# Two weight pieces joined in turn, convolution taps in token halves, and a new step list for the first phase

## The chip, the cores and the metric

The program runs on one core of a Trainium2 chip. Its time is the device time of one execution in microseconds (us). A core has five engines that run side by side, each through its own queue in order: PE (matmul), DVE (vector), ACT (scalar), POOL (GpSimd) and SP (which issues the DMAs here). They wait for one another through semaphores.

## The reference

Attention without a causal mask in two forms (on tokens averaged by 4, and in a local band), their sum as the input of a gated layer, and a mixer over tokens and channels:

```
out_up    = repeat(softmax(q_d k_d^T / 8) v_d, 4)        # q_d, k_d, v_d: means of 4 tokens
out_local = softmax(where(|i-j| < 4, q k^T / 8, -1e9)) v
x   = out_up + out_local                                 # B 4, S 576, 8 heads x 64 = 512 channels
gate = sigmoid(sum_k conv_w[k] * x shifted by 4-k tokens)  # 5 taps per channel
y   = (gate * (x @ w_val)) @ w_out                       # 512 x 512 each
u   = y + (relu(y^T @ w_tok1) @ w_tok2)^T                # tokens 576 -> 256 -> 576
out = u + relu(u @ w_ch1) @ w_ch2                        # channels 512 -> 1536 -> 512
```

The seven weight arrays (`w_val`, `conv_w`, `w_out`, `w_tok1`, `w_tok2`, `w_ch1`, `w_ch2`) arrive as the bits of 64-bit floats.

## The kernel before, in words

Channels lie on the partitions, tokens along the free dimension. A product is made of three fp32r matmuls (L278 to L280, `mm3`): each operand is split into a high and a low part, the high part by a copy on ACT, the low part by a subtraction on DVE (or POOL).

**Weights.** A weight comes in pieces of 128 x 256. `fetch_bits` loads the 64-bit words of a piece into one of three raw buffers (tag `w64`, `NWD` = 3). `join_bits` makes fp32 bits of it with three DVE instructions, each of which reads what the one ahead wrote: a shift and mask (L152), the sign (L153), the low word (L155). Then ACT writes the high part and DVE the low part.

**First phase** (`start`, batch 0). The attention of batch 0, its convolution and the 16 pieces of `w_val` (0 to 7) and `w_out` (8 to 15; an even piece holds columns 0 to 255 of a row block, an odd one the others) run by the string `ORDER`. Each word of it is a step with a number: `qk`, `va`, `vw`, `wf`, `cwf` are loads on SP; `wj` joins a piece, `wl` makes its low part, `S` sums tokens by 4, `md`/`ml` take maxima, `rd`/`rl` normalise, `xf` adds the two attention outputs into x, `ca`/`cb`/`cc` are convolution taps, `xl` the low part of x (all on DVE); `wh`, `ed`, `ela`, `elb`, `cd`, `cl`, `up`, `g`, `xh`, `sg` are on ACT; `D`, `L`, `T`, `O` are on PE, and `z` puts in dummy matmuls that keep PE going. PE, ACT, DVE and SP follow this list word for word. A matmul `p_val` (x times `w_val`) of batch 0 follows the list, and DVE multiplies its result with the gate (`y`, L749); the `p_x` matmuls (y times `w_out`) come next, and need the 16th piece's low part in the end.

**Later phases.** Only PE's order is written out there (`mix` places side work such as attention of batches 1 to 3 and weight steps between the products, by nominal times on PE); the other engines follow a scheduler's priorities. `ch1_new` prepares `w_ch1` (24 pieces, 12 columns blocks `f`), `load_w` the token weights, `ch2_new` prepares `w_ch2` (24 pieces). The convolution of batches 1 to 3 is `conv`: one multiplication (L457) and four taps (L462), each over all 576 tokens and each reading the sum that the tap ahead wrote.

Of the kernel before, what the change touches and what calls it, by code (L numbers as in the profile page):

```python
# [21 lines left out]
NHP = H // 2  # L22
# [15 lines left out]
LAG = 2  # L38
# [15 lines left out]
NW0, NW1 = 8, 3  # L54
# [5 lines left out]
TAG0 = {"sc_d": "as", "sc_l": "m", "o_d": "n", "o_l": "n"}  # L60
# [25 lines left out]
def kernel(ctx, tc, qk, vw, v4, w_val, conv_w, w_out, w_tok1, w_tok2, w_ch1, w_ch2, out):  # L86
# [32 lines left out]
    def busy(n):  # L119
        for _ in range(n):  # L120
            p = T(ps, [128, 512], F32, "ao", BANKS["ao"], name="idle_ps")
            nc.tensor.matmul(p, lhsT=idle, rhs=idle.unsqueeze(1).to_broadcast([128, 4, 128]), start=True, stop=True)

# [25 lines left out]
    def join_bits(x, n, rows, full=None):  # L149
        a = T(sb, [128, n], I32, "wa", NWD, name="wa")[0:rows]  # L150
        low, high = x[:, :, 0], x[:, :, 1]
        nc.vector.tensor_scalar(a, high, 3, 0x3FFFFFF8, ALU.logical_shift_left, ALU.bitwise_and)  # L152
        nc.vector.scalar_tensor_tensor(out=a, in0=high, scalar=-0x40000000, in1=a,  # L153
                                       op0=ALU.bitwise_and, op1=ALU.bitwise_or)
        nc.vector.scalar_tensor_tensor(out=a if full is None else full.bitcast(I32), in0=low, scalar=29, in1=a,  # L155
                                       op0=ALU.logical_shift_right, op1=ALU.bitwise_or)
        return a

    def decode(src, n, rows, hi, lo, shape=None, keep=0, lo_eng=nc.vector):
        a = join_bits(fetch_bits(src, n, rows, shape), n, rows)  # L160

        def split():
            nc.scalar.activation(out=hi, in_=a.bitcast(F32), func=AF.Copy)
            lo_eng.tensor_tensor(out=lo, in0=a.bitcast(F32), in1=hi.bitcast(F32), op=ALU.subtract)  # L164

        if not keep:
            flush()
        pending.append(split)

    def load_w(key, pieces, tag, bufs, parts=None):  # L170

        for j, group in enumerate(pieces):
            n = group[0][1].shape[1]
            hi, lo = parts or [T(sb, [128, len(group), n], F32R, tag, bufs, name=f"{key}{j}_{p}") for p in ("hi", "lo")]
            for i, (rows, src) in enumerate(group):
                for c in range(0, n, WB):
                    e = min(n, c + WB)
                    decode(src[:, c:e], e - c, rows, hi[0:rows, i, c:e], lo[0:rows, i, c:e])
                wt[key].append((hi[:, i, :], lo[:, i, :]))
                yield  # L180
# [21 lines left out]
    def ch1_new(f):  # L202
# [41 lines left out]
    def ch2_new():  # L244
# [10 lines left out]
        for k in range(NP):  # L255
            w = wt["ch2", k] = [next(slots) for _ in range(7)]
            x = []
            for f, c in ((k, WB), (k + NP, WB), (k, 0), (k + NP, 0)):
                x.append(whole("pt", NPT))
                join_bits(fetch_bits(w_ch2[f * 128:f * 128 + 128, c:c + WB], WB, 128), WB, 128, full=x[-1])  # L260
                with behind_pace():
                    for _ in range(2):
                        if splits:
                            part(*splits.pop(0))
                yield
# [46 lines left out]
    def softmax(parts, e, scale, mult):  # L312
# [17 lines left out]
        mult.tensor_tensor(out=e, in0=e, in1=bc(sm, w), op=ALU.mult)  # L330

    def attention(b):
# [3 lines left out]
        early = lambda: tc.high_priority(offset=PRI) if b else nullcontext()  # L336
        mult = nc.gpsimd if b else nc.vector

        def bank(shape, name, tag=None):
            if b:  # L340
                tag = "as" if name[:2] == "sc" else "ao"
            else:
                tag = tag or TAG0.get(name, "ao")
            return T(ps, shape, F32, tag, BANKS[tag], name=name)

        def sums(hp):
# [7 lines left out]
            if b == 0:  # L354
                d["vd"] = [w[:, r] for r in range(4)]
                return
# [5 lines left out]
        def low_scores(hp):  # L362
# [9 lines left out]
            softmax(parts, e, 0.125 / 16.0, mult)  # L372
# [31 lines left out]
        def loc_scores(hp):  # L404
# [16 lines left out]
            softmax(parts, e, 0.125, mult)  # L421
# [50 lines left out]
        if b:

            hpd[0] = load(b, 0)
            hpd[0]["v"] = load_v(b, 0)
            yield
            sums(0)
            for i in range(NHP + 1):
                if i < NHP:
                    low_scores(i)  # L480
                    yield
                if i:
                    low_turn(i - 1)
                    yield
                if i < NHP:
                    loc_scores(i)
                    yield
                if i + 1 < NHP:
                    hpd[i + 1] = load(b, i + 1)
                    sums(i + 1)  # L490
                if i:
                    low_out(i - 1)
                    yield
                    loc_turn(i - 1)
# [544 lines left out]
```

## Time and profile before

| | |
|---|---|
| median of 3 runs | 645.43 us (643.77 to 650.33) |
| profiled execution | 649.24 us, of which the span is 647.5 us |
| PE busy | 594.6 us, 92% of the span |
| DVE busy | 461.0 us, 71% |
| ACT / POOL busy | 338.5 us, 52% / 136.4 us, 21% |

A busy share is a mean over stages with different limits. The first 90 us hold the attention of batch 0 and the first weights; after that PE runs the large products nearly without a break. The profiled execution took 3.8 us more than the median.

### The profile page before, as it was taken

What the parts mean: (1) busy time and instruction counts of PE and PEld (TensorE: products, weight loads), DVE (VectorE), ACT (ScalarE), POOL (GpSimd) and SP (SyncE); (2) the same over time, 40 slices, a digit from 0 to 9 for tenths busy, and PEclk for the clock granted to TensorE, in tenths of its full rate; (3) what the DMA queues carried; (4) which work ended last, traced back from release to release, by engine and by line L of the source; (5) the groups of instructions that cost most, each with busy time, mean ns of one, the idle gap of its engine ahead of it and who ended that gap; (6) DMA issues with size and microseconds to landing.
All of it is one profiled execution on the core that took longest, in us unless ns stands there. A gap on an engine that the chain in (4) does not pass through costs nothing.

```text
span 647.5 us, 13172 instructions
## 1 busy us (share of the span) xinstructions
PE 594.6 (92%) x4995; PEld 540.1 (83%) x4995; DVE 461.0 (71%) x967; ACT 338.5 (52%) x1118; POOL 136.4 (21%) x152
## 2 busy tenths in 40 slices
PE   8878489988887999899999999999998999999997
PEld 4566378777786988899888899898898999999996
DVE  5699988896996379566253666336997968677684
ACT  4567465665455654737646454324453554554542
POOL 1041202244362412614331240410300000000000
PEclk9687687987988999999999999999999999999999
DMA  8931253384766154697234579314699998767642
GB/s 247 264 117 46 65 148 100 107 259 141 247 239 200 56 189 153 222 302 245 83 98 162 161 256 354 132 54 157 205 304 320 334 317 296 253 222 233 232 147 74
DMA packets 79103, 125.34 MB, mean 194 GB/s; under 512 B 6528, under 2 KB 61824, under 8 KB 79040
## 3 DMA queue, kind: packets, MB, share of 16 engines
q1 hardware_dynamic: 79040, 124.51, 59.6%
q8 instruction: 39, 0.64, 0.4%
q14 instruction: 24, 0.20, 0.1%
HBM read 83.99 MB, written 40.50 MB: 192 GB/s over the span
## 4 chain that ended last, share of the span: by engine, by line
PE 59%; DVE 22%; DMA 8%; ACT 6%; issue 2%; POOL 2%; SPq 0%; POOLq 0%; DVEq 0%; ACTq 0%
DMA qk_sb<-in_qk_dram 6%; PE p_o L279 6%; PE p_o L280 6%; PE p_o L278 6%; PE g_ps L278 5%; PE g_ps L279 5%; PE g_ps L280 5%; DVE gate_sb L462 3%; PE sc_l L417 3%; PE p_x L278 2%; PE p_val L278 2%; DVE wa L153 2%; PE p_val L280 2%; PE p_val L279 2%; PE p_x L280 2%
## 5 line engine op out<-in xcount | busy, mean ns | idle before, releaser
L278 PE MATMUL g_ps<-u_hl,w_hl 128*128 128x288 f32 x384 | 117.5, 306 | 3.9 <-DMA w_hl<-w_dr 1.9
L279 PE MATMUL g_ps<-u_hl,w_hl 128*128 128x288 f32 x384 | 114.7, 299 | 3.3 <-POOL u_hl L711 3.1
L280 PE MATMUL g_ps<-u_hl,w_hl 128*128 128x288 f32 x384 | 113.6, 296 | 0.8 <-DVE w_hl L164 0.8
L710 ACT ACTIVATE g_hl<-r_back 128x384 fp32r<-128x384 f32 x126 | 65.8, 526 | 62.3 <-PE p_o L280 55.6
L711 DVE TENSOR_TENSOR g_hl<-r_back,g_hl 128x384 fp32r<-128x384 f32 x126 | 68.0, 556 | 32.3 <-ACT g_hl L710 31.0
L279 PE MATMUL p_o<-g_hl,ch_w 128*128 128x384 f32 x252 | 84.9, 337 | 1.0 <-DVE g_hl L711 0.6
L280 PE MATMUL p_o<-g_hl,ch_w 128*128 128x384 f32 x252 | 84.7, 336 | 0.0
L278 PE MATMUL p_o<-g_hl,ch_w 128*128 128x384 f32 x252 | 84.6, 336 | 0.0
L278 PEld LDWEIGHTS g_ps<-u_hl,w_hl 128*128 128x128 f32 x384 | 72.5, 189 | 7.7 <-issue 2.9
L279 PEld LDWEIGHTS g_ps<-u_hl,w_hl 128*128 128x128 f32 x384 | 72.7, 189 | 4.9 <-POOL u_hl L711 4.8
L280 PEld LDWEIGHTS g_ps<-u_hl,w_hl 128*128 128x128 f32 x384 | 72.8, 190 | 1.0 <-DVE w_hl L164 1.0
L866 ACT ACTIVATE r_sb<-g_ps 128x288 f32<-128x288 f32 x96 | 38.8, 408 | 64.0 <-PE g_ps L280 55.6
L870 DVE TENSOR_TENSOR r_sb<-r_sb 128x288 f32<-128x288 f32 x96 | 48.4, 504 | 25.1 <-ACT r_sb L866 23.3
L278 PE MATMUL p_x<-y_hl,out_hi 128*128 128x288 f32 x128 | 41.4, 324 | 8.6 <-ACT out_hi L664 7.7
L279 PEld LDWEIGHTS p_o<-g_hl,ch_w 128*128 128x128 f32 x252 | 47.3, 188 | 2.3 <-DVE g_hl L711 2.3
L462 DVE SCALAR_TENSOR_TENSOR gate_sb<-x_f,cw,gate_sb 128x575 f32<-128x575 f32 (+3 forms) x48 | 48.3, 1006 | 0.5
L278 PEld LDWEIGHTS p_o<-g_hl,ch_w 128*128 128x128 f32 x252 | 47.3, 188 | 0.0
L280 PEld LDWEIGHTS p_o<-g_hl,ch_w 128*128 128x128 f32 x252 | 47.3, 188 | 0.0
L278 PE MATMUL p_val<-x_hl,val_hi 128*128 128x288 f32 x128 | 40.6, 317 | 3.1 <-DVE y L749 3.1
L711 POOL TENSOR_TENSOR u_hl<-u_sb,u_hl 128x288 fp32r<-128x288 f32 x32 | 27.9, 889 | 60.1 <-ACT u_hl L710 60.1
L280 PE MATMUL p_x<-y_hl,out_lo 128*128 128x288 f32 x128 | 39.3, 307 | 1.4 <-DVE out_lo L667 1.4
L711 POOL TENSOR_TENSOR x_hl<-x_f,x_hl 128x288 fp32r<-128x288 f32 x28 | 26.2, 950 | 66.6 <-ACT x_hl L710 55.4
(149 smaller groups left out, 1401.6 us busy)
## 6 DMA issues: line engine op xcount, KB each, us to landing
r_dr<-r_sb SPq DMA_DIRECT2D x24, 1008.0 KB, 5.3
r_back<-r_dr SPq DMA_DIRECT2D x21, 1152.0 KB, 6.1
w_hl<-w_dr SPq DMA_DIRECT2D x27, 512.0 KB, 5.9
w<-in_w_ch_dram SPq DMA_DIRECT2D x48, 256.0 KB, 4.4
qk_sb<-in_qk_dram SPq DMA_DIRECT2D x16, 589.0 KB, 5.0
w_dr<-w_hl SPq DMA_DIRECT2D x12, 512.0 KB, 3.0
v_sb<-in_vw_dram SPq DMA_DIRECT2D x16, 320.0 KB, 4.5
v_sb<-in_v_dram SPq DMA_DIRECT2D x16, 288.0 KB
```

The source lines that it names most:

```text
L153: nc.vector.scalar_tensor_tensor(out=a, in0=high, scalar=-0x40000000, in1=a, op0=ALU.bitwise_and, op1=ALU.bitwise_or)
L278: nc.tensor.matmul(out_ap, lhsT=lh, rhs=rh, start=first, stop=False)
L279: nc.tensor.matmul(out_ap, lhsT=lh, rhs=rl, start=False, stop=False)
L280: nc.tensor.matmul(out_ap, lhsT=ll, rhs=rh, start=False, stop=last)
L417: nc.tensor.matmul(p[r0:r0 + 64, c, :], lhsT=qk[r0:r0 + 64, 0, 3 + o:3 + o + WIN], rhs=qk[r0:r0 + 64, 1, o:o + WIN], start=False, stop=(c ...
L462: nc.vector.scalar_tensor_tensor(out=g[:, t0:s1], in0=x[:, t0 - sh:s1 - sh], scalar=cw[:, hp, k:k + 1], in1=g[:, t0:s1], op0=ALU.mult, op1 ...
L710: nc.scalar.activation(out=hi_ap, in_=src_ap, func=AF.Copy)
L711: lo_eng.tensor_tensor(out=lo_ap, in0=src_ap, in1=hi_ap.bitcast(F32), op=ALU.subtract)
L866: paced[0] = nc.scalar.activation(out=r[:, 2 * (i % 2) + hs], in_=p[:, 0:HS], func=AF.Relu)
L870: nc.vector.tensor_tensor(out=r[:, o], in0=r[:, x], in1=r[:, y], op=ALU.subtract)
```

## The change

1. `join_bits` takes a list of pieces and issues the first instruction for all, then the second for all, then the third for all. `start` joins two pieces per step (`wp`, in the order of `WORD`: 0 to 7, then the even pieces of `w_out`, then the odd ones), `load_w`, `ch1_new` and `ch2_new` join two at a time, with half as many side steps (7 to 6 and 24 to 12). The number of join buffers goes from 3 to 4 (`NWA`); the raw buffers stay 3.
2. A convolution tap becomes two instructions, one for each half of its tokens, and the halves alternate. In `start` a tap over 576 (or 288) tokens is cut in the middle. The multiplication ahead stays whole.
3. `ORDER` is written anew; the number of dummy matmuls goes from 55 to 36.
4. One of the four differences that `c1` takes of its products becomes a sum, so that it no longer reads the result just ahead.

The parts of the code that are left out below only remove what batch 0 no longer uses.

```
+NWA = 4
+WORD = [*range(8), 8, 10, 12, 14, 9, 11, 13, 15]
...
-    def join_bits(x, n, rows, full=None):
...
+    def join_bits(xs, fulls=None):
+        parts = [(x, T(sb, [128, x.shape[1]], I32, "wa", NWA, name="wa")[0:x.shape[0]]) for x in xs]
+        outs = [a if fulls is None else full.bitcast(I32) for (_, a), full in zip(parts, fulls or xs)]
+        for x, a in parts:
+            nc.vector.tensor_scalar(a, x[:, :, 1], 3, 0x3FFFFFF8, ALU.logical_shift_left, ALU.bitwise_and)
+        for x, a in parts:
+            nc.vector.scalar_tensor_tensor(out=a, in0=x[:, :, 1], scalar=-0x40000000, in1=a,
+                                           op0=ALU.bitwise_and, op1=ALU.bitwise_or)
+        for (x, a), o in zip(parts, outs):
+            nc.vector.scalar_tensor_tensor(out=o, in0=x[:, :, 0], scalar=29, in1=a,
+                                           op0=ALU.logical_shift_right, op1=ALU.bitwise_or)
+        return outs
...
             for sh in range(1, TAPS):
-                k, t0 = TAPS - 1 - sh, max(s0, sh)
-                nc.vector.scalar_tensor_tensor(out=g[:, t0:s1], in0=x[:, t0 - sh:s1 - sh], scalar=cw[:, hp, k:k + 1],
-                                               in1=g[:, t0:s1], op0=ALU.mult, op1=ALU.add)
+                k = TAPS - 1 - sh
+                for t0, s1 in ((sh, HS), (HS, S)):
+                    nc.vector.scalar_tensor_tensor(out=g[:, t0:s1], in0=x[:, t0 - sh:s1 - sh], scalar=cw[:, hp, k:k + 1],
+                                                   in1=g[:, t0:s1], op0=ALU.mult, op1=ALU.add)
...
-                        for o, x, y in ((5, 3, 1), (1, 1, 0), (4, 3, 1), (6, 4, 2)):
-                            nc.vector.tensor_tensor(out=r[:, o], in0=r[:, x], in1=r[:, y], op=ALU.subtract)
+                        for o, x, y, op in ((5, 3, 1, ALU.subtract), (1, 1, 0, ALU.subtract), (4, 5, 0, ALU.add),
+                                            (6, 4, 2, ALU.subtract)):
+                            nc.vector.tensor_tensor(out=r[:, o], in0=r[:, x], in1=r[:, y], op=op)
```

On DVE, the first two joins of the program (pieces 0 and 1 of `w_val`, raw buffers 127 and 129). Before:

```order
L152 TENSOR_SCALAR wa_179<-w64_127 128x256
L153 SCALAR_TENSOR_TENSOR wa_179<-w64_127,wa_179 128x256
L155 SCALAR_TENSOR_TENSOR wa_179<-w64_127,wa_179 128x256
L152 TENSOR_SCALAR wa_193<-w64_129 128x256
L153 SCALAR_TENSOR_TENSOR wa_193<-w64_129,wa_193 128x256
L155 SCALAR_TENSOR_TENSOR wa_193<-w64_129,wa_193 128x256
```

Now, at the same place:

```order
L144 TENSOR_SCALAR wa_179<-w64_127 128x256
L144 TENSOR_SCALAR wa_180<-w64_129 128x256
L146 SCALAR_TENSOR_TENSOR wa_179<-w64_127,wa_179 128x256
L146 SCALAR_TENSOR_TENSOR wa_180<-w64_129,wa_180 128x256
L149 SCALAR_TENSOR_TENSOR wa_179<-w64_127,wa_179 128x256
L149 SCALAR_TENSOR_TENSOR wa_180<-w64_129,wa_180 128x256
```

The same six instructions; no instruction reads what the one directly ahead wrote. On DVE, the end of the first phase before, from the last taps of the convolution (the last of seven single joins follow in the same pattern):

```order
L643 SCALAR_TENSOR_TENSOR gate_sb_104<-x_f32_100,cw_91,gate_sb_104 128x288 x3
L152 TENSOR_SCALAR wa_860<-w64_615 128x256
L153 SCALAR_TENSOR_TENSOR wa_860<-w64_615,wa_860 128x256
L155 SCALAR_TENSOR_TENSOR wa_860<-w64_615,wa_860 128x256
L667 TENSOR_TENSOR out0_lo_116<-wa_849,out0_hi_115 128x256
L152 TENSOR_SCALAR wa_871<-w64_747 128x256
L153 SCALAR_TENSOR_TENSOR wa_871<-w64_747,wa_871 128x256
L155 SCALAR_TENSOR_TENSOR wa_871<-w64_747,wa_871 128x256
L667 TENSOR_TENSOR out1_lo_118<-wa_860,out1_hi_117 128x256
```

Now the end of the first phase on DVE reads:

```order
L736 TENSOR_TENSOR y32_978<-p_val_965,gate_sb_104 128x288
L149 SCALAR_TENSOR_TENSOR wa_878<-w64_732,wa_878 128x256
L149 SCALAR_TENSOR_TENSOR wa_879<-w64_823,wa_879 128x256
L628 SCALAR_TENSOR_TENSOR gate_sb_104<-x_f32_100,cw_91,gate_sb_104 128x144
L698 TENSOR_TENSOR y_hl_913<-y32_978,y_hl_913 128x288
L628 SCALAR_TENSOR_TENSOR gate_sb_104<-x_f32_100,cw_91,gate_sb_104 128x144 x7
L654 TENSOR_TENSOR out1_lo_118<-wa_816,out1_hi_117 128x256
L654 TENSOR_TENSOR out3_lo_122<-wa_879,out3_hi_121 128x256
L654 TENSOR_TENSOR out2_lo_120<-wa_878,out2_hi_119 128x256
L654 TENSOR_TENSOR out0_lo_116<-wa_815,out0_hi_115 128x256
```

Six of the eight pieces of `w_out` are joined ahead of the first `y` now, and all eight ahead of these last taps; four low parts are left for the end. On SP, the loads that the new list moves. Before, from the second load of q and k on:

```order
L291 DMA qk_sb_131<-in_qk_dram 128x1178
L297 DMA v4_sb_133<-in_v4_dram 72x1024
L306 DMA v_sb_135<-in_vw_dram 128x640
L143 DMA w64_137<-in_w_val_dram 128x512
L291 DMA qk_sb_183<-in_qk_dram 128x1178
L297 DMA v4_sb_185<-in_v4_dram 72x1024
L306 DMA v_sb_187<-in_vw_dram 128x640
L143 DMA w64_189<-in_conv_w_dram 128x40
L291 DMA qk_sb_191<-in_qk_dram 128x1178
L297 DMA v4_sb_197<-in_v4_dram 72x1024
L306 DMA v_sb_199<-in_vw_dram 128x640
L143 DMA w64_201<-in_w_val_dram 128x512
```

Now, from the third load of q and k on (the second and piece 2 stand ahead of it):

```order
L288 DMA qk_sb_135<-in_qk_dram 128x1178
L294 DMA v4_sb_137<-in_v4_dram 72x1024
L303 DMA v_sb_139<-in_vw_dram 128x640
L133 DMA w64_187<-in_conv_w_dram 128x40
L133 DMA w64_189<-in_w_val_dram 128x512
L288 DMA qk_sb_191<-in_qk_dram 128x1178
L294 DMA v4_sb_193<-in_v4_dram 72x1024
L303 DMA v_sb_195<-in_vw_dram 128x640
L288 DMA qk_sb_1087<-in_qk_dram 128x1178
L133 DMA w64_318<-in_w_val_dram 128x512
L288 DMA qk_sb_1225<-in_qk_dram 128x1178
L133 DMA w64_320<-in_w_val_dram 128x512
```

The values of heads 4 to 7 (`v4`, `vw`) are loaded later, q, k and piece 3 (`w64_189`, before `w64_201`) earlier; the loads of batch 1's q and k (1087, 1225) now stand ahead of pieces 4 and 5 (318, 320).

## Rows read from the trace of the kernel before

**Rows 1.** The page: each engine's busy time, and TensorE's granted clock in 40 slices.

```profile
PE 594.6 (92%) x4995; PEld 540.1 (83%) x4995; DVE 461.0 (71%) x967; ACT 338.5 (52%) x1118; POOL 136.4 (21%) x152
PEclk9687687987988999999999999999999999999999
```

**Rows 2.** Busy us (and instructions) of each engine in stretches; clock, DMA share, GB/s.

```profile
4.59:32.00 27.41, 23.70 (x234) 15.07 (x232) 19.32 (x41) 15.46 (x82) 0.00 (x0) 0.81 0.98 272
32.00:83.81 51.81, 36.97 (x427) 29.53 (x424) 50.15 (x104) 31.75 (x114) 12.21 (x12) 0.77 0.27 82
...
68.60:80.77 12.17, 3.10 (x7) 1.88 (x8) 11.60 (x28) 5.49 (x15) 3.65 (x4) 0.58 0.30 87
...
88.68:260.00 171.32, 152.63 (x1443) 134.18 (x1441) 136.00 (x283) 96.81 (x382) 57.02 (x53) 0.93 0.52 167
260.00:648.00 388.00, 372.85 (x2856) 355.57 (x2855) 251.04 (x529) 191.18 (x538) 64.14 (x71) 1.00 0.66 215
```

**Rows 3.** Waits up to 100 us: total, times, longest.

```profile
PE p_x L278 <- ACT out_hi L664: 7.7, 2, 6.7
...
ACT out_hi L664 <- DVE wa L155: 6.4, 7, 1.0
...
DVE wa L152 <- DMA w<-in_conv_w_dram: 2.7, 1, 2.7
...
DVE mx L561 <- PE sc_d L534: 2.0, 1, 2.0
```

**Rows 4.** DVE's timeline: start, us, line, shapes [idle before]; single joins.

```profile
6.98 0.29 DVE L152 TENSOR_SCALAR wa<-w 128x256 int32<-128x256 int32 x1
7.30 0.43 DVE L153 SCALAR_TENSOR_TENSOR wa<-w,wa 128x256 int32<-128x256 int32 x1
7.76 0.42 DVE L155 SCALAR_TENSOR_TENSOR wa<-w,wa 128x256 int32<-128x256 int32 x1
8.11 0.88 DVE L561 TENSOR_REDUCE mx<-sc_l 128x6 f32<-128x384 f32 x2
```

**Rows 5.** DVE's timeline at 129 us: two joins that the scheduler put side by side.

```profile
129.04 0.48 DVE L152 TENSOR_SCALAR wa<-w 128x256 int32<-128x256 int32 x2
...
130.79 0.74 DVE L164 TENSOR_TENSOR w_hl<-wa,w_hl 128x256 fp32r<-128x256 f32 x2
```

**Rows 6.** DVE's timeline: taps over 576 tokens, then one over 288.

```profile
47.74 1.66 DVE L643 SCALAR_TENSOR_TENSOR gate_sb<-x_f,cw,gate_sb 128x575 f32<-128x575 f32 x2
49.32 0.17 DVE L578 RECIPROCAL sm<-sm 72x4 f32<-72x4 f32 x1
...
65.98 0.51 DVE L643 SCALAR_TENSOR_TENSOR gate_sb<-x_f,cw,gate_sb 128x286 f32<-128x286 f32 x1
66.41 0.45 DVE L711 TENSOR_TENSOR y_hl<-y,y_hl 128x288 fp32r<-128x288 f32 x1
```

**Rows 7.** DVE's timeline: waits for loads, and the last low part of the first phase.

```profile
10.27 1.35 DVE L525 TENSOR_REDUCE qk_d<-qk_sb 128x288 f32<-128x1152 f32 x1 [0.95 <-DMA qk_sb<-in_qk_dram]
...
24.70 0.29 DVE L152 TENSOR_SCALAR wa<-w 128x256 int32<-128x256 int32 x1 [1.41 <-DMA w<-in_w_val_dram]
...
83.38 0.43 DVE L667 TENSOR_TENSOR out_lo<-wa,out_hi 128x256 fp32r<-128x256 f32 x1
```

**Rows 8.** PE's timeline: first p_val, first stalled p_x, last p_x of the first half.

```profile
61.92 0.30 PE L279 MATMUL p_val<-x_hl,val_hi 128*128 128x288 f32 x1
...
76.10 0.61 PE L278 MATMUL p_x<-y_hl,out_hi 128*128 128x288 f32 x1 [6.74 <-ACT out_hi L664]
...
88.26 0.29 PE L279 MATMUL p_x<-y_hl,out_hi 128*128 128x288 f32 x1
88.39 0.29 PE L280 MATMUL p_x<-y_hl,out_lo 128*128 128x288 f32 x1
```

**Rows 9.** A wait of DVE for a piece of w_ch1; the page's line of these loads.

```profile
198.48 0.29 DVE L152 TENSOR_SCALAR wa<-w 128x256 int32<-128x256 int32 x1 [1.55 <-DMA w<-in_w_ch_dram]
...
w<-in_w_ch_dram SPq DMA_DIRECT2D x48, 256.0 KB, 4.4
```

More of the change, by code (lines that the diff above doesn't have):

```diff
@@ L37 @@
 NW = 16
-LAG = 2
 NE = 4
@@ L117 @@
     nc.vector.memset(idle, 0.0)
[L119 to L122, printed above, removed]
     wt = {k: [] for k in ("val", "out", "tok1", "tok2")}
@@ L147, in fetch_bits, with decode, split @@
         return x
-    def join_bits(x, n, rows, full=None):
[L150 to L162, printed above, removed]
+    def join_bits(xs, fulls=None):
[10 more added lines that the diff above has]
+        return outs
+    def decode(*chunks, shape=None):
+        xs = [fetch_bits(src, n, rows, shape) for src, n, rows, _, _ in chunks]
+        joined = join_bits(xs)
+        def split(a, hi, lo):
             nc.scalar.activation(out=hi, in_=a.bitcast(F32), func=AF.Copy)
[L164 to L168, printed above, removed]
+            nc.vector.tensor_tensor(out=lo, in0=a.bitcast(F32), in1=hi.bitcast(F32), op=ALU.subtract)
+        flush()
+        for a, (_, _, _, hi, lo) in zip(joined, chunks):
+            pending.append(lambda a=a, hi=hi, lo=lo: split(a, hi, lo))
     def load_w(key, pieces, tag, bufs, parts=None):
@@ L257, in ch2_new @@
             x = []
-            for f, c in ((k, WB), (k + NP, WB), (k, 0), (k + NP, 0)):
-                x.append(whole("pt", NPT))
-                join_bits(fetch_bits(w_ch2[f * 128:f * 128 + 128, c:c + WB], WB, 128), WB, 128, full=x[-1])
+            for c in (WB, 0):
+                two = [whole("pt", NPT) for _ in range(2)]
+                join_bits([fetch_bits(w_ch2[f * 128:f * 128 + 128, c:c + WB], WB, 128) for f in (k, k + NP)], two)
+                x += two
                 with behind_pace():
-                    for _ in range(2):
+                    for _ in range(4):
                         if splits:
@@ L335, in attention, with bank @@
         hpd = {}
[L336 to L343, printed above, removed]
+        early = lambda: tc.high_priority(offset=PRI)
+        def bank(shape, name):
+            tag = "as" if name[:2] == "sc" else "ao"
             return T(ps, shape, F32, tag, BANKS[tag], name=name)
@@ L467, in sigmoid @@
+        def sigmoid(hps):
             for hp in hps:
-                with tc.issue_after((behind or paced[0]).ins):
-                    g = g_t[hp][:, s0:s1]
+                with tc.issue_after(paced[0].ins):
+                    g = g_t[hp]
                     nc.scalar.activation(out=g, in_=g, func=AF.Sigmoid)
[L472 to L494, printed above, removed]
-                    yield
-                    loc_out(i - 1)
-                    conv(i - 1)
-                    yield
-                if i + 1 < NHP:
-                    hpd[i + 1]["v"] = load_v(b, i + 1)
-            sigmoid(hps=range(NHP - 1))
-            last_gate[b] = lambda: sigmoid(hps=(NHP - 1,))
-            return
@@ new lines, in attention @@
+        hpd[0] = load(b, 0)
+        hpd[0]["v"] = load_v(b, 0)
+        yield
+        sums(0)
+        for i in range(NHP + 1):
+            if i < NHP:
+                low_scores(i)
+                yield
+            if i:
+                low_turn(i - 1)
+                yield
+            if i < NHP:
+                loc_scores(i)
+                yield
+            if i + 1 < NHP:
+                hpd[i + 1] = load(b, i + 1)
+                sums(i + 1)
+            if i:
+                low_out(i - 1)
+                yield
+                loc_turn(i - 1)
+                yield
+                loc_out(i - 1)
+                conv(i - 1)
+                yield
+            if i + 1 < NHP:
+                hpd[i + 1]["v"] = load_v(b, i + 1)
@@ L505, in start @@
+        sigmoid(hps=range(NHP - 1))
+        last_gate[b] = lambda: sigmoid(hps=(NHP - 1,))
     def start():
@@ L658, in w_fetch, with w_join @@
             t["w", c] = fetch_bits(chunks[c][0], WB, 128)
-        def w_join(c):
-            t["w", c] = join_bits(t["w", c], WB, 128)
+        def w_join(p):
+            two = WORD[2 * p:2 * p + 2]
+            for c, a in zip(two, join_bits([t["w", c] for c in two])):
+                t["w", c] = a
         def w_hi(c):
@@ L988 @@
     a = [None] + [attention(b) for b in range(1, B)]
-    side = [(chain(w_t1(), w_t2()), 7, *T_AT)]
+    side = [(chain(w_t1(), w_t2()), 6, *T_AT)]
     side += [(a[b], NA, *A_AT[b]) for b in range(1, B)]
     last = c2()
-    side += [(ch2_new(), 24, *W2_AT), (last, 1, C2_AT, C2_AT + 1)]
+    side += [(ch2_new(), 12, *W2_AT), (last, 1, C2_AT, C2_AT + 1)]
     with tc.manual_schedule(engines={mybir.EngineType.PE}):
```

65 lines of the change are left out of this document (28 added, 37 removed).

## The prediction

> **What bounds the kernel now.** I read the page first, then the stretches, then the waits and the timelines. The page gives PE 92% and DVE 71% of the span [rows 1], but the granted clock stays at full speed only after the first third, so the loss lies early. The stretches say the same: from 260 us on PE is busy 372.85 of 388 us and DVE 251; from 88.68 to 260 PE is busy 152.6 of 171.3 us [rows 2]. An edit on DVE can win little there. Between 32 and 83.81 us DVE is busy 50.15 of 51.81 us while PE, dummy matmuls included, is busy 37; from 68.6 to 80.77 PE works 3.1 of 12.2 us at a granted clock of 0.58 [rows 2]. The waits name the chain: p_x waits for a high part of `w_out` on ACT (7.7 us), ACT for the third join instruction on DVE (6.4 us) [rows 3]. So the first phase is set by DVE's list, and it ends when DVE has made the last low part of `w_out`, at 83.38 + 0.43 = 83.8 us [rows 7]; the first half's last p_x ends at 88.39 + 0.29 = 88.7 us [rows 8]. Everything after stands behind that.
>
> Ahead of 32 us the limit is another: DVE is busy 19.3 of 27.4 us, the DMA engines 98% at 272 GB/s [rows 2], and DVE stands idle for q and k (0.95 us), `conv_w` (2.7), a piece of `w_val` (1.41) and scores from PE (2.0) [rows 3, 7]; with three waits of 0.60, 0.26 and 0.15 us these make about 8.05 us of DVE waits between 4.6 and 83.8 us.
>
> **The joins.** A single join takes three starts: 6.98, 7.30, 7.76, and the next instruction starts at 8.11 [rows 4]: 0.32 + 0.46 + 0.35 = 1.13 us. The third instruction, on which nothing ahead waits, lets its follower in 0.35 us after its own start; the second, whose follower reads it, only after 0.46. Two joins side by side take 130.79 - 129.04 = 1.75 us [rows 5] where two single ones take 2.26: 0.5 us saved by a pair. Of the 16 pieces of the first phase some 14 were joined without a stranger in between, so 7 x 0.5 = 3.5 us go from DVE's list. All of it counts while DVE is the limit; if the whole list waited for loads it would count nothing. In the later phases the scheduler had put many joins side by side already [rows 5]; I count nothing for them.
>
> The Trainium skill (VectorE: DVE Perf Modes, section The DRAIN you can't avoid) says that the next vector operation starts only when the pipe has emptied, with or without dependence, and advises fewer operations rather than fewer waits. Here 0.35 us from start to start with an instruction of 0.42 us [rows 4] speak against it. By that rule the joins save nothing and the halves cost more; it is a rival below.
>
> **The taps.** Two dependent taps over 576 tokens took 49.32 - 47.74 = 1.58 us up to the next start; a tap over 288 lets its follower in after 66.41 - 65.98 = 0.43 us [rows 6]. Four halves in turn take 4 x 0.43 = 1.72 us: 0.14 us more per two taps, because a second fixed cost is paid where a dependence of about 0.1 us was saved. Six such pairs (heads 0 to 2) add 0.8 us. The last head's taps over 288 become taps over 144, which no row shows; from 0.81 us at 575 and 0.51 at 286 columns I estimate 0.28 us from start to start, 0.56 for both against 0.43 to 0.55 before, so at most 0.1 us on 8 taps, half of which stood dependent: 0.5 us. Sum 1.3 us more on DVE. In batches 1 to 3 the 48 taps cost up to 2 x 0.43 - 0.73 = 0.13 us each, 6.2 us of DVE, 2.1 of it before 190 us. DVE is busy 136 of 171 us there [rows 2], so I take nothing on the path, with 2.1 as upper end.
>
> **The list.** The waits of 8.05 us go or are replaced. `conv_w` is now joined behind the third token sum, when it has long landed; piece 3 is loaded ahead of the fourth q and k and no longer behind the values. New waits: the second token sum is reached earlier (after the pair at about 8.7 us), while its load lands at 10.27 as before: 1.6 us. The third sum now follows closely, its load stands some 2.6 MB deep in the queue (by the page a load of q and k is 589 KB, a piece 256, the values 288 and 320): about 1 us. The pair of pieces 4 and 5 is worst: piece 5 stands behind the loads of batch 1's q and k, 6.46 MB deep, and at 272 GB/s [rows 2] that is 23.7 us after the first issue at 2 us, so 25.8; piece 3 of the old list, 5.35 MB deep, was joined only at 24.70 after a wait [rows 7], 2.9 us later than the same sum gives. So 25.8 to 28.7, and DVE's own work reaches that pair at about 24.8: I take 2.3 us. After that DVE has all its loads. Three waits of 4.9 us in place of 8.05.
>
> At the end there is a new kind of wait. Six of the eight pieces of `w_out` are now made ahead of the first `y`, so only about 10 us of DVE work stand behind the last part of x, and p_val has no dummy matmuls directly ahead of it. PE ran p_val at full clock after twelve dummies and p_x at half speed (0.61 us against 0.29) after the gap at 76 us [rows 8]. Cold, the three `y` after the first would keep DVE waiting 1 to 5 us; I take 2. New waits in all: 6.9 us, with 2.6 and 12 as ends (only the first two waits; the worst load time, a cold PE and about 3 us of chains through PE and ACT that I do not see).
>
> The dummy matmuls, 55 before and 36 now, stand on PE, which DVE keeps waiting; they count only through the clock. The changed sum in `c1` takes one dependence of 0.1 us off DVE 24 times, behind PE's products: nothing.
>
> **The sum.** DVE's last low part: 83.8 - 3.5 + 1.3 - 8.05 + 6.9 = 80.45 us. Before, PE still had 4.9 us of p_x behind it (88.7 - 83.8), partly at half clock. Now the products of the first 256 columns have their weights before and only the second 24 matmuls remain: p_x at full clock starts every 0.133 us (88.39 - 88.26) [rows 8], 3.2 us, with the tail of the last 3.4. End of the half: 83.9 instead of 88.7, a gain of 4.8 us. All that follows moves with it. Profiled 649.24 - 4.8 = 644.4; in proportion for the median 645.43 x (1 - 4.8/649.24) = **640.7 us**.
>
> **The rivals.**
> - *The list wins more.* New waits are only 2.6 us and PE stays warm: 4.3 us more, a gain of 9.1, **636.4 us**. For it: from 32 us on the old list left DVE nothing to wait for [rows 2], and the new one may not either. Against: in the old list unseen waits on PE's scores cost 2 us [rows 3].
> - *New waits take the place of the old.* New waits of 10 us (a cold p_val among them) and 2.1 us for the halves of batch 1: 4.8 - 3.1 - 2.1 = -0.4 us, **645.8 us**. For it: the DMA engines are 98% busy up to 32 us whatever the order [rows 2]; the bytes do not change.
> - *Slower: pairs starve on three raw buffers.* A pair needs two of three; its second load is issued only when the pair ahead has been joined, and these loads take 4.4 us to land in the median [rows 9]. DVE's queue is in order, so what stands behind the join (`y`, x and r parts for PE) waits too. If each of the 12 pairs of `w_ch1` waits as the one piece at 198 us did, 1.55 us [rows 9], that is 18.6 us; DVE is idle 20% of that stretch [rows 2], which leaves 14.8 us: **655.5 us**. It decides from the point where a pair's turn comes sooner than a landing after the pair ahead. Against it: most pairs lie about 10 us apart; only six follow PE's products directly, 24 x 0.133 = 3.2 us apart.
> - *Alternation saves nothing.* Then the 3.5 us of the joins fall away and each half tap costs its full 0.51 us and a gap, 12 x (1.10 - 0.79) - 0.8 = 2.9 us more: 4.8 - 6.4 = -1.6, **647.0 us**. The sentence of the Trainium skill above stands for it, rows 4 and 5 against it.
>
> **How the numbers follow.** Forecast 0.38, more 0.28, taken by new waits 0.20, starved 0.10, nothing saved 0.04. About 1% (6.5 us) is what a measurement of this kernel tells from no change. Faster by over 1% (below 639.0): the second case and the lower quarter of the first, 0.28 + 0.10 = 0.38. Slower by over 1%: the starved case, 0.11 with a rest for what I do not see. Within: 0.51. The range reaches from a little below the second case to above the third and fourth, where 2 in 10 are left out: 634.5 to 648.
>
> **What would show it.** Right: six instructions of a pair of joins within 1.8 us; four half taps in about 1.7 us; DVE's last low part of `w_out` at 78 to 83 us and the last p_x of that half 3.4 us later; the gap of 6.7 us on PE gone; DVE's wait for `conv_w` gone and one for a piece of `w_val` near 25 us in its place. Wrong: pairs of `w_ch1` that wait for loads between 120 and 260 us, a p_val at half speed with DVE waiting for it, or a stretch from there to the end that is not as long as before (559 us from 88.7 to 647.5): then the halves of the taps or the joins act where I counted nothing.

## The result, and the profile after

Forecast: 640.7 us, 4.8 us less. Measured, in 20 runs of each kernel: before 649.15 us in the median, after 648.12; the means are level (648.03 and 647.92 us). The ratio on record, 1.0054 with a 95% interval from 1.0027 to 1.0080, leaves out as slow every run over 1.5% above the fastest of its kernel, and since one run of before was very fast (637.94 us), that takes out 12 of the 20 runs of before and one of the changed kernel; so it shows no loss. A second timing (run c0 below), in which nothing is left out, gave 1.0022 [0.9990, 1.0053]. So the change gains nothing that can be told, and a loss of up to 3 us isn't excluded. The 4.8 us of the forecast are missing.

The page of the changed kernel, busy times and granted clock (against [rows 1]):

```profile
PE 596.2 (92%) x4976; PEld 543.4 (83%) x4976; DVE 461.3 (71%) x1035; ACT 338.1 (52%) x1118; POOL 134.8 (21%) x152
PEclk9957878998797999899999999999999899999999
```

Its execution took 653.2 us. Stretches of the changed kernel (columns as in [rows 2]; the first phase on DVE ends at 77.83 us now, the first half's p_x at 83.18):

```profile
4.59:32.00 27.41, 21.71 (x265) 15.13 (x264) 23.14 (x50) 17.08 (x88) 1.30 (x2) 0.96 0.92 283
32.00:77.83 45.83, 35.33 (x379) 28.08 (x377) 44.99 (x114) 29.69 (x108) 13.23 (x11) 0.72 0.28 92
83.18:260.00 176.82, 155.60 (x1448) 136.46 (x1448) 139.04 (x311) 98.21 (x384) 55.27 (x54) 0.91 0.49 160
260.00:651.00 391.00, 374.62 (x2848) 357.46 (x2847) 249.74 (x549) 190.26 (x535) 61.95 (x69) 0.99 0.65 214
```

The window up to 260 us is longer by the 5.5 us that the first phase won, but PE does only five matmuls more in it (1448 against 1443), and the 289th matmul of c1 (`g_ps`), soon after it, starts at 272.26 us where it started at 272.55: the gain is gone by then. Single executions differ, though: in c0, the same kernel, the half ended at 85.1 us and that matmul starts at 269.1. In the first phase itself the signs are there. DVE's timeline of the changed kernel:

```profile
15.47 0.49 DVE L144 TENSOR_SCALAR wa<-w 128x256 int32<-128x256 int32 x2
15.87 0.76 DVE L146 SCALAR_TENSOR_TENSOR wa<-w,wa 128x256 int32<-128x256 int32 x2
16.54 0.76 DVE L149 SCALAR_TENSOR_TENSOR wa<-w,wa 128x256 int32<-128x256 int32 x2
17.21 0.17 DVE L562 RECIPROCAL sm<-sm 72x4 f32<-72x4 f32 x1
...
25.90 0.29 DVE L144 TENSOR_SCALAR wa<-w 128x256 int32<-128x256 int32 x1 [3.15 <-DMA w<-in_w_val_dram]
...
47.97 1.78 DVE L628 SCALAR_TENSOR_TENSOR gate_sb<-x_f,cw,gate_sb 128x285 f32<-128x285 f32 x4
49.68 0.48 DVE L144 TENSOR_SCALAR wa<-w 128x256 int32<-128x256 int32 x2
...
76.41 1.42 DVE L654 TENSOR_TENSOR out_lo<-wa,out_hi 128x256 fp32r<-128x256 f32 x4
```

A pair of joins takes 17.21 - 15.47 = 1.74 us, four half taps 1.71 us; the wait for a piece of `w_val` stands at 25.90 us; the last low part is made at 76.41 + 1.42 = 77.83 us, where it was 83.8 [rows 7].

PE's timeline: the first p_val, the p_x that waits for the last low parts, and the half's last p_x (against [rows 8]):

```profile
62.62 0.40 PE L275 MATMUL p_val<-x_hl,val_hi 128*128 128x288 f32 x1 [1.61 <-DVE x_f L618]
62.86 0.29 PE L276 MATMUL p_val<-x_hl,val_hi 128*128 128x288 f32 x1
62.99 0.29 PE L277 MATMUL p_val<-x_hl,val_lo 128*128 128x288 f32 x1
...
77.89 0.61 PE L277 MATMUL p_x<-y_hl,out_lo 128*128 128x288 f32 x1 [2.28 <-DVE out_lo L654]
78.29 0.44 PE L275 MATMUL p_x<-y_hl,out_hi 128*128 128x288 f32 x1
...
82.88 0.29 PE L277 MATMUL p_x<-y_hl,out_lo 128*128 128x288 f32 x1
```

The wait of 6.74 us is now one of 2.28; behind it p_x runs at half clock for ten products (0.24 us from start to start, then 0.13; the granted clock is 0.50 from 77.9 to 80.6 us), so the tail takes 5.3 us. The half ends at 83.2 us instead of 88.7. In the twelve other executions with this list (c0, e1 to e4, h2, h4, d1, d2, b1, g1, g2) it ended at 81.8 to 85.1, and in h1, which has the list of before, at 86.9.

### The profile page after: what moved, and what is told of

Same layout as the page of the kernel before. It is cut to its first block, busy times and chain, and to the rows that moved or that the text cites. A ratio compares the mean times of both kernels' runs of the same rounds, so it can differ in the third digit from the quotient of the medians.

```text
span 651.4 us, 13201 instructions
## 1 busy us (share of the span) xinstructions
PE 596.2 (92%) x4976; PEld 543.4 (83%) x4976; DVE 461.3 (71%) x1035; ACT 338.1 (52%) x1118; POOL 134.8 (21%) x152
## 4 chain that ended last, share of the span: by engine, by line
PE 53%; DVE 30%; ACT 7%; DMA 6%; issue 3%; SPq 0%; POOL 0%; ACTq 0%; DVEq 0%
PE p_o L276 6%; PE p_o L277 6%; PE p_o L275 6%; DVE gate_sb L450 4%; PE g_ps L275 4%; PE g_ps L276 4%; PE g_ps L277 4%; DVE r_sb L858 3%; PE sc_l L407 3%; DVE gate_sb L628 3%; DVE wa L146 2%; PE p_x L275 2%; DMA w<-in_w_val_dram 2%; DVE wa L144 2%; PE p_x L277 2%
## 5 line engine op out<-in xcount | busy, mean ns | idle before, releaser
L275 PE MATMUL g_ps<-u_hl,w_hl 128*128 128x288 f32 x384 | 119.4, 311 | 6.6 <-DVE u_sb L815 3.1
L276 PE MATMUL g_ps<-u_hl,w_hl 128*128 128x288 f32 x384 | 115.6, 301 | 1.0 <-POOL u_hl L698 0.8
L277 PE MATMUL g_ps<-u_hl,w_hl 128*128 128x288 f32 x384 | 114.9, 299 | 0.0
L275 PEld LDWEIGHTS g_ps<-u_hl,w_hl 128*128 128x128 f32 x384 | 73.9, 192 | 11.1 <-issue 8.5
L276 PEld LDWEIGHTS g_ps<-u_hl,w_hl 128*128 128x128 f32 x384 | 74.1, 193 | 2.2 <-POOL u_hl L698 2.2
L277 PEld LDWEIGHTS g_ps<-u_hl,w_hl 128*128 128x128 f32 x384 | 74.0, 193 | 0.0
L450 DVE SCALAR_TENSOR_TENSOR gate_sb<-x_f,cw,gate_sb 128x287 f32<-128x287 f32 (+3 forms) x96 | 52.6, 613 | 0.2
L275 PE MATMUL p_x<-y_hl,out_hi 128*128 128x288 f32 x128 | 40.9, 320 | 1.2 <-ACT u_sb L749 0.6
L276 PE MATMUL p_x<-y_hl,out_hi 128*128 128x288 f32 x128 | 38.9, 304 | 1.1 <-DVE y_hl L698 1.1
```

The lines of the kernel that those rows point to most:

```text
L275: nc.tensor.matmul(out_ap, lhsT=lh, rhs=rh, start=first, stop=False)
L276: nc.tensor.matmul(out_ap, lhsT=lh, rhs=rl, start=False, stop=False)
L277: nc.tensor.matmul(out_ap, lhsT=ll, rhs=rh, start=False, stop=last)
```

## The experiments

All were timed beside the kernel before, in five rounds. Medians in us, ratio with its 95% interval (0.001 is 0.65 us). A ratio is uncertain by some 2 to 3 us, a difference of two by some 3 to 4:

| run | what it is | this | before | ratio |
|---|---|---|---|---|
| c0 | the changed kernel again | 648.20 | 647.17 | 1.0022 [0.9990, 1.0053] |
| e1 | changed, whole taps in batches 1 to 3 | 640.36 | 646.16 | 0.9916 [0.9884, 0.9949] |
| e2 | changed, `w_ch2` joined singly | 647.68 | 646.16 | 1.0031 [1.0004, 1.0059] |
| e3 | changed, token weights and `w_ch1` joined singly | 649.21 | 646.16 | 1.0035 [1.0003, 1.0067] |
| e4 | only the first phase and the buffer changed | 637.10 | 646.16 | 0.9869 [0.9838, 0.9901] |
| h1 | before, half taps in batches 1 to 3 | 652.15 | 646.63 | 1.0104 [1.0067, 1.0140] |
| h2 | changed, half taps in batch 1, whole in 2 and 3 | 644.62 | 646.63 | 0.9963 [0.9925, 1.0002] |
| f1 | e4, first phase joined singly | 641.91 | 646.63 | 0.9923 [0.9887, 0.9959] |
| f2 | e4, first phase with whole taps | 639.07 | 646.63 | 0.9868 [0.9820, 0.9917] |
| h4 | changed, half taps ranked lower | 639.92 | 646.69 | 0.9921 [0.9884, 0.9958] |
| d1 | e1 and 48 idle products | 650.71 | 646.69 | 1.0094 [1.0055, 1.0134] |
| d2 | d1, taps and idle products ranked lower | 642.56 | 645.86 | 0.9962 [0.9934, 0.9991] |
| b1 | e4, whole taps ranked lower | 640.40 | 646.69 | 0.9907 [0.9874, 0.9940] |
| p1 | before, four buffers for joined pieces | 643.13 | 646.69 | 0.9932 [0.9896, 0.9967] |
| q1 | e4 with three buffers | 642.09 | 645.86 | 0.9941 [0.9914, 0.9967] |
| g1 | e1 and e3 together | 636.20 | 647.17 | 0.9838 [0.9791, 0.9885] |
| g2 | e1 and e2 together | 638.17 | 647.17 | 0.9874 [0.9822, 0.9926] |

**Which part takes the gain back: e1, e2, e3, e4.** Theory one: the half taps of batches 1 to 3. Rivals: the pairs of `w_ch2`, whose loads come earlier; the pairs of the other weights, which starve; a chain behind the first phase that gives back any gain.

```
 e1, in conv:
-                for t0, s1 in ((sh, HS), (HS, S)):
-                    nc.vector.scalar_tensor_tensor(out=g[:, t0:s1], ...
+                nc.vector.scalar_tensor_tensor(out=g[:, sh:S], in0=x[:, 0:S - sh], ...
 e2, in ch2_new:
-            for c in (WB, 0):
...
+            for f, c in ((k, WB), (k + NP, WB), (k, 0), (k + NP, 0)):
...
 e3, in load_w and ch1_new: decode one chunk a time, 7 steps instead of 6
 e4: e1, e2 and e3 together, and the old four differences in c1
```

> The changed kernel with the taps of batches 1 to 3 whole again (48 instead of 96). If the half taps there cost what the first phase gained (5.07 us for three halves at 137.6 behind a run of GpSimd operations), the time falls by 3 to 5 us against the changed kernel, ratio to before 0.993 to 0.996. If they are not the cause, it stays within 1 us of the changed kernel, 0.998 to 1.002.

> The changed kernel with the pieces of w_ch2 joined one by one in 24 steps, as before. If the pairs move loads of raw pieces ahead of the last load of w1 and so cost 2.5 us of PE's wait at 507 us, c2's first g_hl comes 2.5 to 3.8 us earlier and the ratio to before is about 0.995. If that wait was chance or comes from elsewhere, it is within 1 us of the changed kernel, 0.998 to 1.002.

> The changed kernel with the pieces of w_tok1, w_tok2 and w_ch1 joined one by one (7 steps for the token weights, one fetch and one join at a time), as before. If pairs starve on three raw buffers, the wait of 2.2 us for w_ch1 at 197 and the PE wait of 5.03 us behind it go, and the time falls by 2 to 4 us (ratio to before 0.994 to 0.997). If not, within 1 us of the changed kernel, 0.998 to 1.002.

> Only the first phase is changed (new list, pairs and halves there); everything behind it is written as before. If what was gained at the end of the first phase (5.5 us at the second u copies, 83.22 against 88.72) moves all that follows, the ratio to the kernel before is 0.992 to 0.994 (4 to 5.5 us less). If the gain is given back whatever stands behind it (a chain between 130 and 290 us that does not start earlier when the first phase ends earlier), the ratio is 0.998 to 1.002 and the offset of u_sb<-p_h and r_sb against the trace of before shrinks to below 1 us by 290 us.

Whole taps bring 1.0022 down to 0.9916, some 6.9 us; undoing either of the pairs alone brings nothing. The chain that gives back any gain falls with e4. The expectation of e2 came from the profiles: at the last phase's fourth high part on ACT (`g_hl`) before and the changed kernel were 0.4 us apart (475.24 and 475.62 us), at its sixth 3.6 (511.67 and 515.27). In c0, the same kernel, these two start at 472.34 and 509.21 us, nearly as far from one another as before, so that loss was chance.

**The halves by themselves: h1, h2.** h1 puts the two lines of `conv` into the kernel before; h2 takes halves `if b == 1 else ((sh, S),)`.

> The kernel before with one edit: the taps of batches 1 to 3 (not those of the first phase) as alternating halves. If the halves there cost by themselves what they cost in the changed kernel (run e1: about 7 us, the difference between 640.4 and the 647.7 and 649.2 of the two runs beside it that keep the halves), the ratio is 1.007 to 1.012. If they cost only beside the new first phase, which shifts them into a run of GpSimd operations, it is 0.998 to 1.003.

> The changed kernel with halves in batch 1 and whole taps in batches 2 and 3. The traces of the changed kernel and of run e1 part between 88 and 200 us, where batch 1's taps lie, and keep their distance after 260 us: so this run should be as slow as the changed kernel, ratio 0.999 to 1.004. If the cost is spread evenly over the 96 halves, two thirds of it go and the ratio is about 0.994 to 0.996.

h1: 1.04%, 6.7 us, with the old first phase too. h2 is 3.0 us slower than e1, with a third of the halves; that goes with a cost spread over the batches, and not with one in batch 1 alone, as I had expected.

**Time or place: h4, d1, d2.** The traces show what stands behind the taps. DVE in the changed kernel, batch 1: the end of a head's x (L442), eight half taps (L450), then the maxima (L316) for the next head's low scores:

```profile
114.15 0.82 DVE L442 TENSOR_TENSOR x_f<-o_l,x_f 128x290 f32<-128x290 f32 x2 [2.90 <-PE o_l L436]
115.01 0.52 DVE L446 TENSOR_SCALAR gate_sb<-x_f,cw 128x576 f32<-128x576 f32 x1
115.57 2.85 DVE L450 SCALAR_TENSOR_TENSOR gate_sb<-x_f,cw,gate_sb 128x287 f32<-128x287 f32 x5
118.34 0.68 DVE L760 TENSOR_TENSOR x_hl<-x_ps,x_hl 128x512 fp32r<-128x512 f32 x1
118.94 1.36 DVE L450 SCALAR_TENSOR_TENSOR gate_sb<-x_f,cw,gate_sb 128x288 f32<-128x288 f32 x3
120.22 0.80 DVE L316 TENSOR_REDUCE mx<-sc_d 72x2 f32<-72x288 f32 x2
```

The same place in e1, with whole taps:

```profile
111.16 0.52 DVE L446 TENSOR_SCALAR gate_sb<-x_f,cw 128x576 f32<-128x576 f32 x1
111.71 1.43 DVE L449 SCALAR_TENSOR_TENSOR gate_sb<-x_f,cw,gate_sb 128x575 f32<-128x575 f32 x1
113.07 0.44 DVE L316 TENSOR_REDUCE mx<-sc_d 72x2 f32<-72x288 f32 x1
113.44 0.80 DVE L449 SCALAR_TENSOR_TENSOR gate_sb<-x_f,cw,gate_sb 128x574 f32<-128x574 f32 x1
114.16 0.44 DVE L316 TENSOR_REDUCE mx<-sc_d 72x2 f32<-72x288 f32 x1
```

Between dependent whole taps the scheduler lets in other work, the maxima first: they come 1.9 us after the multiplication (L446) starts, with halves 5.2 us (2.0 in h4 and 5.3 in d1, below). In the second head of batch 1 it is the sums of u (L815), which the c1 products wait for. DVE's timeline of the changed kernel:

```profile
137.22 0.44 DVE L815 TENSOR_TENSOR u_sb<-p_h,u_sb 128x288 f32<-128x288 f32 x1
137.59 5.07 DVE L450 SCALAR_TENSOR_TENSOR gate_sb<-x_f,cw,gate_sb 128x287 f32<-128x287 f32 x3
142.58 0.45 DVE L815 TENSOR_TENSOR u_sb<-p_h,u_sb 128x288 f32<-128x288 f32 x1
```

POOL's timeline at the same time, and PE's behind it:

```profile
136.93 1.51 POOL L348 TENSOR_TENSOR v_sb<-v_sb 72x512 f32<-72x512 f32 x1
138.40 1.47 POOL L327 TENSOR_TENSOR e_l<-e_l,sm 128x640 f32<-128x640 f32 x1
139.84 0.79 POOL L698 TENSOR_TENSOR u_hl<-u_sb,u_hl 128x288 fp32r<-128x288 f32 x1
140.59 0.79 POOL L698 TENSOR_TENSOR x_hl<-x_f,x_hl 128x288 fp32r<-128x288 f32 x1
141.34 1.00 POOL L698 TENSOR_TENSOR u_hl<-u_sb,u_hl 128x288 fp32r<-128x288 f32 x1
```

```profile
143.17 0.37 PE L275 MATMUL g_ps<-u_hl,w_hl 128*128 128x288 f32 x1 [2.30 <-DVE u_sb L815]
```

h4 leaves the 96 halves and gives them a lower rank; d1 leaves the taps whole and fills the pauses between them; d2 is d1 with the lower rank:

```
 h4, at the call of conv:
+                with tc.high_priority(offset=-600):
+                    conv(i - 1)
 d1, behind each tap, which is whole as in e1:
+                nc.vector.tensor_scalar(idle, x[:, 0:128], cw[:, hp, k:k + 1], None, ALU.mult)
```

> The changed kernel with all its half taps, but the taps of batches 1 to 3 rank 600 places lower with the scheduler, so that the maxima of the next scores and the sums of u come ahead of them on VectorE (in batch 1 the maxima of the second head's low scores stand behind the second half tap instead of the eighth). Order theory (alternating halves leave no hole in which the scheduler would put maxima and sums, so these stand behind blocks of eight taps): most of the 7 us come back, ratio to before 0.990 to 0.996. Time theory (6.2 us more of VectorE work is on the path wherever it stands): ratio 1.000 to 1.005 as in the changed kernel.

> Run e1 (whole taps in batches 1 to 3, ratio 0.992) with an idle product over 128 columns behind each of the 48 taps, whose result nobody reads. It fills the holes between the dependent taps as the second halves do, so the maxima come behind the taps again. By both theories it is slower than e1; it gives the size: if VectorE's time counts (an instruction of about 0.15 us each, up to 5 us more), ratio 0.996 to 1.000; if the order alone costs as much as the halves did, 1.000 to 1.005; if neither counts and it is a matter of 0.5 us instructions held up by GpSimd, 0.990 to 0.994.

> Run d1 (whole taps and 48 idle products, ratio 1.009) with the lower rank of run h4 for taps and idle products. Order theory: the maxima and sums come ahead again and the time of VectorE costs little, ratio 0.991 to 0.996 (run e1 without idle products: 0.992). Time theory: the idle products cost on the path wherever they stand, ratio 1.004 to 1.009.

The same place in h4, and then in d1:

```profile
112.13 0.52 DVE L446 TENSOR_SCALAR gate_sb<-x_f,cw 128x576 f32<-128x576 f32 x1
112.69 1.56 DVE L450 SCALAR_TENSOR_TENSOR gate_sb<-x_f,cw,gate_sb 128x287 f32<-128x287 f32 x2
114.17 0.81 DVE L316 TENSOR_REDUCE mx<-sc_d 72x2 f32<-72x288 f32 x2
```

```profile
112.62 0.52 DVE L446 TENSOR_SCALAR gate_sb<-x_f,cw 128x576 f32<-128x576 f32 x1
113.06 0.28 DVE L452 TENSOR_SCALAR idle<-x_f,cw 128x128 bf16<-128x128 f32 x1
113.25 1.36 DVE L449 SCALAR_TENSOR_TENSOR gate_sb<-x_f,cw,gate_sb 128x575 f32<-128x575 f32 x1
...
117.90 0.44 DVE L316 TENSOR_REDUCE mx<-sc_d 72x2 f32<-72x288 f32 x1
```

With the halves left in but behind the maxima, 0.9921: as fast as with whole taps (e1, 0.9916). With whole taps and the pauses filled, 1.0094: 11.5 us slower than e1 (9.8 by the medians), from 48 x 0.19 = 9.1 us of idle products (0.19 us from start to start); the lower rank takes 8.5 us of that back (d2, 0.9962) and leaves 3 us. So the place costs, and the time of DVE costs little (halves: nothing that can be told; idle products: a third of it). The rank is no gain in itself: with whole taps and nothing in the pauses (b1 below) it brings nothing. And d1 has no half taps, so half taps that POOL holds up (last section) are not needed for the loss. The path goes through the low scores' maxima: ACT waits for them before its exponentials, and PE's queue stops at the next local scores until ACT has read the low ones. PE's wait there from 84 to 265 us (total, times, longest), for before:

```profile
PE sc_l L411 <- ACT e_d L325: 5.1, 3, 2.6
```

For e1, where another wait at the same matmuls is put down to a join:

```profile
PE sc_l L401 <- DVE wa L144: 3.7, 1, 3.7
...
PE sc_l L401 <- ACT e_d L322: 3.0, 3, 1.8
```

For h1:

```profile
PE sc_l L411 <- ACT e_d L325: 12.6, 5, 5.2
```

For the changed kernel:

```profile
PE sc_l L401 <- ACT e_d L322: 13.0, 5, 5.0
```

For d1:

```profile
PE sc_l L401 <- ACT e_d L322: 14.9, 5, 4.7
```

For h4, whose profiled execution took 645.8 us (its median is 639.9):

```profile
PE sc_l L401 <- ACT e_d L322: 8.8, 2, 7.0
```

For d2:

```profile
PE sc_l L401 <- ACT e_d L322: 7.8, 2, 6.1
```

In all seven the longest of these waits lies at 187 to 200 us, where the maxima come directly behind joins of `w_ch1`, with whatever taps. Without that one the sums are 2.5 us before, 3.0 in e1, 1.8 in h4 and 1.7 in d2, against 7.4 in h1, 8.0 in the changed kernel and 10.2 in d1. So some 5 us of the 7 show as these waits; where the rest lies isn't shown.

**The buffer: p1, q1.** p1 sets the join buffers of the kernel before from 3 to 4; q1 sets those of e4 from 4 to 3 and puts one `wl11` ahead of `wp7`.

> The kernel before with four buffers instead of three for joined pieces, and nothing else. If a part of what run e4 won behind the first phase (8.5 us in the end, 5.5 to 6.9 at the second u copies) comes from the fourth buffer in the token and w_ch1 weights, ratio 0.994 to 0.997; otherwise 0.998 to 1.002.

> Run e4 (only the first phase changed, ratio 0.987) with three buffers for joined pieces as before; for that one low part of w_out moves ahead of the last pair of joins. If the fourth buffer and the first phase add up (run p1: the buffer alone gives 0.993), this run keeps only the first phase's part, ratio 0.992 to 0.995, which is the prediction's 4.8 us by itself. If the buffer's gain in run p1 needs the old first phase, ratio 0.986 to 0.989.

The fourth buffer alone gives 0.9932, 4.4 us, and without it e4's first phase gives 0.9941, 3.8 us; the product, 0.9873, is e4's 0.9869. ACT's waits for joined pieces from 88 to 205 us, before and then in p1:

```profile
ACT w_hl L163 <- DVE wa L155: 9.1, 5, 3.2
ACT tok_hl L163 <- DVE wa L155: 3.6, 2, 2.3
```

```profile
ACT tok_hl L164 <- DVE wa L156: 3.2, 1, 3.2
ACT w_hl L164 <- DVE wa L156: 2.7, 2, 1.6
```

12.7 us become 5.9. The gain shows between the first half's end and the 289th matmul of c1: 183.9 us before and 175.5 in p1, 183.5 in q1 and 176.2 in e4. That the shorter waits for joined pieces bring it is likely but not shown, since ACT's waits for parts of x and u grew in p1.

**The terms of the first phase: f1, f2.** f1 joins the two pieces of a step one behind the other, f2 leaves the taps of the first phase whole.

> Run e4 (only the first phase changed, ratio 0.987) with its pieces joined one behind the other in the same places of the list, three instructions for one and then three for the next. The prediction's term: seven pairs save 0.5 us each on a DVE that sets the end of the phase, so 3.5 us are lost, ratio about 0.992, and the last low part of w_out comes 3 to 3.5 us later. If DVE's waits for loads take up what pairs save ahead of 26 us, 1.5 to 2.5 us, ratio 0.989 to 0.991.

> Run e4 with the taps of the first phase whole, so that no tap of the kernel is halved. The prediction's term: the halves add 1.3 us to DVE there, so this run is 1 to 1.5 us faster, ratio about 0.985, with the last low part of w_out 1.3 us earlier. If halves are worth it beside dependent whole taps, it is slower than e4 (0.987).

f1 loses 0.0054, 3.5 us, and its last low part is made at 81.0 us instead of 76.2 in e4; from the first join to there DVE is busy 70.0 us instead of 66.6. f2 is as fast as e4 and its last low part is made at 76.4, though DVE is busy 1.6 us less (65.0): in f2's profile DVE waits 2.6 us for p_val, which ran at half clock (granted clock 0.50 from 62 to 66 us), and in e4's it doesn't. So the halves there cost DVE work, and what they cost in time can't be told from that wait.

**What is left, and the best version: b1, g1, g2, c0.**

> Run e4 (only the first phase changed, ratio 0.987) with the same lower rank for the taps of batches 1 to 3, which are whole here. If maxima and sums behind taps still cost something with whole taps, 2 to 4 us less than e4, ratio 0.981 to 0.984, the fastest version; if the holes had let them through already, 0.985 to 0.989.

> Run e1 (whole taps in batches 1 to 3, ratio 0.992) with single joins for w_tok1, w_tok2 and w_ch1 too; pairs stay in the first phase and for w_ch2. If the pairs of these weights make up the distance between e1 (0.992) and e4 (0.987), ratio 0.985 to 0.989; if it is chance or the pairs of w_ch2, 0.990 to 0.993.

> Run e1 (0.992) with single joins for w_ch2 in 24 steps; pairs stay elsewhere. If the pairs of w_ch2 make up the distance between e1 and e4 (0.987), ratio 0.985 to 0.989; otherwise 0.990 to 0.993. With both runs at 0.990 to 0.993, the pairs behind the first phase cost nothing that can be told.

> The changed kernel as it is, on the chip of these runs. From the parts (first phase alone 0.9941, fourth buffer 0.9932, halves in batches 1 to 3 1.0104, and the distance from e4 to e1 1.005 for the later pairs) the product is 1.002; the first timing gave 1.0054 with an interval from 1.0027 to 1.0080. If parts add up, 0.999 to 1.006.

A lower rank brings nothing more to whole taps. The product of the parts, 0.9941 x 0.9932 x 1.0104, is 0.998, and with the distance of e1 from e4 1.002; c0 measured 1.0022. That agreement is closer than the parts are known. Where that distance (3 us) comes from isn't settled: it goes with either of the pairs undone (g1, g2), the intervals of e1 and g2 overlap, and with half taps neither shows (e2, e3). The sum in `c1`, which e4 takes back, is not the reason, since g1 and g2 keep it. The fastest versions have the new first phase, four buffers, whole taps in batches 1 to 3, and single joins in some or all of the later weights: g1, e4, g2 and f2, at 0.984 to 0.987, 8 to 10 us below the kernel before.

## Why the prediction was wrong, point by point

- **Joins, 3.5 us: right.** f1 measured 3.5 us of time and 3.4 us of DVE work. The rival by which alternation saves nothing falls with it. The section of the Trainium skill on which that rival leaned (VectorE: DVE Perf Modes, section The DRAIN you can't avoid) states the rule for operations with and without a semaphore between them, and adds, which the prediction left out, that an operation that is not held starts earlier. So these did: two of 0.42 us that don't depend on one another start 0.34 us apart (0.76 us for both, at 16.54 us above).
- **Taps of the first phase, 1.3 us more: right as work, not told in the time.** DVE is busy 1.6 us more in e4's list than in f2's; a wait for p_val in f2 hides it.
- **New waits, 6.9 us: mis-sized.** DVE's waits of over 0.3 us from its first join to 77.83 us were 0.36, 3.15 and 0.62 us. The piece of `w_val` cost 3.15 where I took 2.3 (1.2 to 5.2 in the twelve other executions of this list, mostly about 2); the second token sum (1.6 taken), the third (1) and p_val (2) brought none here, though p_val brought 2.1 in e2 and 1.1 in e3. PE was at full clock from its second p_val on. DVE's list ended at 77.8, not 80.45 us. The tail on PE took 5.3 us, not 3.4, since p_x ran at half clock behind its wait. The two misses nearly cancel, by luck: the half ended 5.5 us earlier where 4.8 were forecast, and q1 puts the first phase by itself at 3.8 us of the whole time.
- **The 48 taps of batches 1 to 3, "I take nothing on the path, with 2.1 as upper end": the step that failed.** They cost 6.9 us (c0 against e1; h1: 6.7), which alone is more than the gain that was forecast. The 6.2 us of DVE work were sized rightly (busy 461.0 before, 467.2 in h1), and DVE's idle share did hide nearly all of them, as h4 shows. What I did not ask is what the halves do to the order: where a scheduler sets it, they close the pauses in which maxima and sums of u had passed the taps, and PE stands behind those.
- **The fourth buffer: left out of the sum.** I told of it in the change and gave it no term. It gives 4.4 us.
- **"All that follows moves with it": right for the first phase, as e4 and q1 show,** and with the two terms above the changes nearly cancel: -3.8 - 4.4 + 6.9 and some 3 us not settled make +1.7 us; c0 measured +1.4. Each of these parts is uncertain by 2 to 3 us or more.
- **Starved pairs: not the 14.8 us of the rival.** DVE's waits for pieces of `w_ch1` and `w_ch2` grew from 3.9 us before to 9.0 in sum (one of 2.2 at 196.9 us against the 1.55 of [rows 9]), but with single joins for the token weights and `w_ch1` (e3) they are 5.9 and the time stayed. With whole taps, single joins go with 5 us less (g1 against e1, on different chips, the intervals just touching), so a small cost isn't excluded.

The last sign that the prediction named, a stretch from the first half's end to the end that isn't as long as before, was the one that came: 568 us in the profile (560 in c0's) against 559.

## What to carry to other kernels

Where a scheduler orders an engine's queue, cutting one dependent chain into two that alternate also closes the pauses through which other work passed: look at what stands behind the chain in the new order, and who waits for it, before counting only the chain's own time. If that work matters more, rank it ahead; then the cut itself cost nothing that could be told here. And every constant in a diff needs a term: one more buffer was worth about as much as the whole new list.

## What the runs showed that I had not expected

Three half taps of 0.5 us each took 5.07 us while POOL ran five operations back to back from 136.93 to 142.34 us. The Trainium skill (SBUF — State Buffer, section Who interferes with whom) says that DVE and GpSimd share one pair of ports, which one operation holds to its end while the other waits in full; a DVE operation with two inputs in SBUF, as a tap is, contends there with a GpSimd operation that reads SBUF. The trace agrees: the three taps end at 138.76, 141.70 and 142.66 us, each 0.32 us behind the end of a POOL operation, and three of those ended while the second tap waited. So a block of DVE instructions that falls into such a run holds up what is queued behind it some three times as long as its own 1.5 us say.
